# Decode attention: P times V spread over four column strips of TensorE, heads folded by four matmuls

## The chip, the cores and the metric

The kernel runs on one core of a Trainium2 chip. The core has TensorE (PE, with its weight loads shown apart as PEld), VectorE (DVE), ScalarE (ACT), GpSimd (POOL), SyncE (SP, which only issues transfers here) and 16 DMA engines that bring data from HBM into SBUF, the on-chip memory of 128 partitions. Matmul results land in PSUM, a second memory of 128 partitions with eight banks of 512 fp32 columns each. The metric is the device time of one execution in microseconds, lower is better.

## The reference

One token is decoded. Two branches share the input x (1 x 512) and are mixed by a gate:

```python
g = sigmoid((x * gate_w).sum(-1, keepdims=True))
# A: attention over a cache, H = 32 heads, Sk = 65536 positions, Dh = 128
q = (x @ wq) split into heads
p = softmax(q . k_cache * Dh**-0.5)
a = (p @ v_cache, heads side by side) @ wo
# B: feed-forward, F = 1792
b = (silu(x @ w_gate) * (x @ w_up)) @ w_down
out = g * a + (1 - g) * b
```

All tensors are bf16. The K and V caches are 512 MiB each, and every byte of them is needed once; all the weights together are some 13 MB.

## The kernel before

**Tiling.** Of each head's 65536 positions, partition p holds positions 512p to 512p + 511, so a head is 512 columns of positions, "blocks", each with 128 values. `CUTS` divides them into three tiles of 168, 168 and 176 blocks, 96 tiles in all (N = 32 x 3) for K and 96 for V. A tile is 5,376 or 5,632 KB. Four ring slots in SBUF (`SLOTS`, line 18) hold whatever K and V tiles are in flight or in work; a slot's next load waits until the last reader of the slot's old tile is done.

**Order.** Everything is issued in an order written out by hand (`manual_schedule`, line 80; the loop from line 555 and the tail from line 608). SP issues all loads (`load`, line 139, the transfer itself at line 147). A step n of the loop loads K tile n and a V tile v that lags by three to five tiles (`LEAD`, `SKIPS`), and then issues, per engine in this order:

- if a head's last V tile was done in the step before: the head's sum of P times V (`head_diagonal`);
- the products of K with q on DVE (`products`: line 304 multiplies in place, line 308 adds halves until 16 columns are left);
- in the first step of a head, in the middle of the DVE work, the previous head's maximum, its spread over the partitions by a matmul (line 363), and its exponentials on ACT (line 374), which write P_sb, 128 x 512 in bf16;
- the head's row (`head_row`), which scales the 128 sums by the gate over the softmax's total and puts them into a row;
- P times V for tile v (`values`, line 401): one matmul for every four blocks, 42 or 44 in a tile;
- the rest of the score sums (`scores`, line 325: PE adds the 16 columns over an identity matrix), after which the K slot is free.

**P times V.** For blocks j to j+3 the stationary operand is P_sb[:, j:j+4] (128 x 4) and the moving operand is the four blocks of V (128 x 512). The 4 x 512 result in PSUM holds P of block c' times V of block c; only c = c' is wanted, that is, row c in columns 128c to 128c + 127. All 128 matmuls of a head add into the same four partitions of one bank, and two such banks take turns by head.

**A head's sum.** For 30 of the heads `head_diagonal` copies the four wanted pieces to SBUF with four activations, each of which multiplies its 4 x 128 columns by a column of the identity (zeroing the other rows); one fp32 matmul with ones adds the four partitions into a row of 512, and DVE adds its four parts of 128 (line 444). For the last two heads `head_copy` and `head_column` bring the unmasked 4 x 512 to SBUF and pick the rows with four matmuls against columns of the identity, giving a column.

**The end.** After the last step the remaining V tiles arrive in smaller pieces (`V_CUTS`), then the tiles of wo (`load_wo`, line 237); `project` (line 513) multiplies the heads' sums by wo as its pieces arrive, one activation copies the result and SP stores it.

Of the kernel before, what the change touches and what calls it, by code (L numbers as in the profile page):

```python
# [8 lines left out]
ACT = mybir.ActivationFunctionType  # L9
ALU = mybir.AluOpType  # L10
AXIS = mybir.AxisListType
P = 128
# [23 lines left out]
def kernel(  # L36
# [14 lines left out]
    nc = tc.nc  # L51
    bf16 = mybir.dt.bfloat16
    f32 = mybir.dt.float32

    _, H, Sk, Dh = A_k_cache.shape
# [5 lines left out]
    NBH = Sk // P  # L61
# [4 lines left out]
    scale = float(Dh) ** -0.5  # L66
# [4 lines left out]
    consts = ctx.enter_context(tc.tile_pool(name="consts", bufs=1))  # L71
    small = ctx.enter_context(tc.tile_pool(name="small", bufs=2))
    ppool = ctx.enter_context(tc.tile_pool(name="ppool", bufs=2))
    psum_s = ctx.enter_context(tc.tile_pool(name="psum_s", bufs=2, space=bass.MemoryType.PSUM))
    psum_o = ctx.enter_context(tc.tile_pool(name="psum_o", bufs=2, space=bass.MemoryType.PSUM))
    psum_a = ctx.enter_context(tc.tile_pool(name="psum_a", bufs=1, space=bass.MemoryType.PSUM))
    psum_r = ctx.enter_context(tc.tile_pool(name="psum_r", bufs=1, space=bass.MemoryType.PSUM))
    psum_m = ctx.enter_context(tc.tile_pool(name="psum_m", bufs=2, space=bass.MemoryType.PSUM))
# [20 lines left out]
    ident_f = consts.tile([P, P], f32, name="ident_f")  # L99
# [3 lines left out]
    ones_f = consts.tile([P, P], f32, name="ones_f")  # L103
# [7 lines left out]
    for t in range(KT):  # L111
        nc.tensor.matmul(
            x_ps[:, t : t + 1],
            lhsT=x_row.rearrange("o (p t) -> o t p", t=KT)[:, t, :],
            rhs=one_b,
            start=True,
            stop=True,
        )
    nc.scalar.activation(out=xT, in_=x_ps, func=ACT.Copy)
    for t in range(KT):  # L120
        nc.vector.tensor_copy(out=X_bc[:, t, :], in_=xT[:, t : t + 1].to_broadcast([P, P]))

    rowsum = consts.tile([P, 1], f32, name="rowsum")
    oT = consts.tile([P, 2 * H + 1], bf16, name="oT")
    nc.vector.memset(oT, 0.0)
# [4 lines left out]
    rg = consts.tile([P, H], f32, name="rg")  # L130
    a_ps = psum_a.tile([1, D], f32, name="a_ps")

    S_parts = {}
    K_tiles, V_tiles, S_tiles, P_tiles, O_tiles = {}, {}, {}, {}, {}

    def span(n):
        return CUTS[n % G], CUTS[n % G + 1]

    def load(dst, cache, n, name, cuts=None):
        h = n // G  # L140
        a, b = span(n)
        t, taken[name, n] = big(name)
        view = t[:, : (b - a) * Dh].rearrange("p (j d) -> p j d", d=Dh)
        src = cache[0, h, :, :].rearrange("(p j) d -> p j d", p=P)
        cuts = cuts or (0, b - a)
        for c, d in zip(cuts[:-1], cuts[1:]):
            nc.sync.dma_start(out=view[:, c:d, :], in_=src[:, a + c : a + d, :])
        dst[n] = view
# [30 lines left out]
    WG = 4  # L179
# [157 lines left out]
    def add_up(n):  # L337

        h = n // G
        a, b = span(n)  # L340
        if a == 0:
            S_tiles[h] = consts.tile([P, NBH], f32, name="S_sb")
        nc.vector.tensor_reduce(  # L343
            out=S_tiles[h][:, a:b], in_=S_parts.pop(n), axis=AXIS.X, op=ALU.add
        )
# [47 lines left out]
    def values(n, lo=0, hi=None):  # L393

        h = n // G
        a, b = span(n)
        hi = b - a if hi is None else hi
        if a + lo == 0:
            O_tiles[h] = psum_o.tile([4, 4 * Dh], f32, name="O_ps")
        for j in range(lo, hi, 4):  # L400
            nc.tensor.matmul(  # L401
                O_tiles[h],
                lhsT=P_tiles[h][:, a + j : a + j + 4],
                rhs=V_tiles[n][:, j : j + 4, :],
                start=(a + j == 0),
                stop=(a + j == NBH - 4),
            )
        if hi == b - a:
            del V_tiles[n]
            free.append(taken.pop(("V_t", n)))  # L410

    def head_copy(h):
        O_ps = O_tiles.pop(h)
        O_sb = small.tile([4, 4 * Dh], f32, name="O_sb")
        nc.scalar.activation(out=O_sb, in_=O_ps, func=ACT.Copy)
        return [O_sb[:, c * Dh : (c + 1) * Dh] for c in range(4)]

    def head_column(h, O_parts):
        oh_ps = psum_m.tile([P, 1], f32, name="oc_ps", tag="misc")
        for c in range(4):  # L420
            nc.tensor.matmul(
                oh_ps, lhsT=O_parts[c], rhs=ident_f[0:4, c : c + 1], start=(c == 0), stop=(c == 3)
            )
        nc.scalar.activation(
            out=oT[:, 2 * h + 1 : 2 * h + 2], in_=oh_ps, func=ACT.Copy, scale=rg[:, h : h + 1]
        )

    def head_diagonal(h):
        O_ps = O_tiles.pop(h)
        O_sb = small.tile([4, 4 * Dh], f32, name="O_sb")  # L430
        for c in range(4):
            nc.scalar.activation(  # L432
                out=O_sb[:, c * Dh : (c + 1) * Dh],
                in_=O_ps[:, c * Dh : (c + 1) * Dh],
                func=ACT.Copy,
                scale=ident_f[0:4, c : c + 1],
            )
        r_ps = psum_r.tile([1, 4 * Dh], f32, name="r_ps")
        nc.tensor.matmul(r_ps, lhsT=ones_f[0:4, 0:1], rhs=O_sb, start=True, stop=True)  # L439
        return r_ps  # L440

    def head_row(h, r_ps):
        r_sb = consts.tile([1, Dh], f32, name="r_sb")
        nc.vector.tensor_reduce(  # L444
            out=r_sb, in_=r_ps.rearrange("o (c d) -> o d c", c=4), axis=AXIS.X, op=ALU.add
        )
        if h < WG:
            for a, b, s, at in pieces:
                lo, hi = max(a, h * Dh), min(b, h * Dh + Dh)
                if lo < hi:  # L450
                    nc.scalar.activation(
                        out=tall_rows[s][:, at + lo - a : at + hi - a],
                        in_=r_sb[:, lo - h * Dh : hi - h * Dh],
                        func=ACT.Copy,
                        scale=rg[0:1, h : h + 1],
                    )
            return
        if h % WG == 0:
            rows[h // WG] = small.tile([1, WG * Dh], bf16, name="o_row")
        at = (h % WG) * Dh  # L460
        nc.scalar.activation(  # L461
            out=rows[h // WG][:, at : at + Dh], in_=r_sb, func=ACT.Copy, scale=rg[0:1, h : h + 1]
        )

    def turn_first():
# [57 lines left out]
    def fold_copy():  # L523
        a_sb = small.tile([4, 4 * Dh], f32, name="O_sb")[0:1, :]
        nc.scalar.activation(out=a_sb, in_=a_ps, func=ACT.Copy)
        fold["a"] = psum_a.tile([2, D // 2], f32, name="a_ps")
        return a_sb
# [11 lines left out]
    rows = {}  # L539
# [15 lines left out]
    for n, v in steps:  # L555
        if n > 1:
            load(K_tiles, A_k_cache, n, "K_t")
        if v is not None:
            load(V_tiles, A_v_cache, v, "V_t", V_CUTS.get(v))
            for half in range(2):  # L560
                if n - half in TALL_LOADS:
                    load_tall(TALL_LOADS[n - half], half)
            if n == N - 1:
                load(V_tiles, A_v_cache, v + 1, "V_t", V_CUTS.get(v + 1))
        size = span(n)[1] - span(n)[0]
        cuts = (0, size // 2, size) if n == 0 else (0, size)
        top_of = None
        if n % G == 0 and n > 0:
            top_of = n // G - 1
            cuts = (0, 64, size)  # L570
        vector = (i for a, b in zip(cuts[:-1], cuts[1:]) for i in products(n, a, b))
        r_ps = None
        if done is not None:
            r_ps = head_diagonal(done)
        if top_of is not None:
            next(vector, None)
            add_up(top_of * G + G - 1)
            exponentials(top_of, row_max(top_of))
        for _ in vector:
            pass  # L580
        if n == FOLD:
            a_sb = fold_copy()
        if n % G:
            add_up(n - 1)
        if r_ps is not None:
            head_row(done, r_ps)
        if n == 2:
            feed_forward_out(*ff)
        if v is not None:
            values(v)  # L590
        if group is not None:
            (turn if group else lambda g: turn_first())(group)
        if n == 1:
            ff = feed_forward_in()
        scores(n)
        if n == 1:
            ff = feed_forward_mid(*ff)
            free.append(gu_slot)
        if group:
            late.append(group)  # L600
        if n in TALL_PROJECTS:
            project_tall(TALL_PROJECTS[n])
        if n == FOLD:
            fold_in(a_sb)
        group = done // WG if done is not None and done % WG == WG - 1 else None
        done = v // G if v is not None and v % G == G - 1 else None
# [12 lines left out]
    O_parts = head_copy(H - 2)  # L619
# [8 lines left out]
    O_parts = head_copy(H - 1)  # L628
# [39 lines left out]
```

## Time and profile before

| | |
|---|---|
| time, median of 3 runs | 2522.24 us (2522.07 to 2522.47) |
| span of the profiled execution | 2520.4 us |
| PE busy | 1408.6 us (56%), weight loads 488.2 us |
| DVE busy | 2234.4 us (89%) |
| ACT busy | 103.4 us (4%) |
| transfer queue of SP | 1087.65 MB, 99.9% of the 16 engines' span |
| HBM read | 1087.64 MB, 432 GB/s over the span |
| mean granted TensorE clock | 0.734 of full |

The profiled execution's own time is not listed apart from its span; the runs' median is 1.8 us above that span. The span runs from the first to the last instruction. The digits of the page's slices are busy tenths of one fortieth of the span each. In a group's line stand the line of code, the engine, the operation, what it writes and reads, shapes and count, then busy time and the mean of one in ns, and behind the bar the idle time of the engine just before these instructions and what ended it. In the chain of waits each row is a start, a length and what the time went to; a DMA row lasts from the issue of the transfer to its landing, queueing included.

### The profile page before, as it was taken

Reading aid. Unit: us, or ns where it says so; the run is one execution under the profiler, and the core shown is the slowest. Engines: PE = TensorE matmul, PEld = TensorE weight load, DVE = VectorE, ACT = ScalarE, POOL = GpSimd, SP = SyncE. Lnnn points to the kernel's source line nnn. Section 1 sums busy time; section 2 is a strip of 40 time slices with the busy share of each in tenths; the row PEclk is TensorE's granted clock in tenths of the full one; section 3 lists DMA queues with packets and bytes.
Section 4 is the critical chain, followed back from the end, with each engine's and each line's share of the span. In section 5 each row is a group of like instructions: output and inputs, shape, how many; then the busy total and the mean of one; then the engine's idle time right before and its main releaser. Section 6 shows DMA issues by size and latency. Waiting matters only on the chain.

```text
span 2520.4 us, 12122 instructions
## 1 busy us (share of the span) xinstructions
PE 1408.6 (56%) x5174; PEld 488.2 (19%) x5174; DVE 2234.4 (89%) x788; ACT 103.4 (4%) x314; POOL 0.7 (0%) x6
## 2 busy tenths in 40 slices
PE   2555546565555654655546565554564655556468
PEld 1111112121121211211212121111121211112123
DVE  7999998988989889999889998889999889898880
ACT  1000000000000000000000000000000000000000
POOL 0000000000000000000000000000000000000000
PEclk7677767676776766677767777776677777777779
DMA  9999999999999999999999999999999999999999
GB/s 420 430 439 433 433 431 435 431 433 434 434 432 436 433 434 433 432 434 433 431 434 435 435 433 431 434 433 433 433 433 433 436 434 434 433 432 431 434 434 390
DMA packets 31101, 1088.41 MB, mean 432 GB/s; under 512 B 3532, under 2 KB 4048, under 8 KB 5192
## 3 DMA queue, kind: packets, MB, share of 16 engines
q1 hardware_dynamic: 31046, 1087.65, 99.9%
q8 instruction: 40, 0.66, 0.1%
q14 instruction: 13, 0.11, 0.0%
q10 hardware_dynamic: 2, 0.00, 0.0%
HBM read 1087.64 MB, written 0.00 MB: 432 GB/s over the span
## 4 chain that ended last, share of the span: by engine, by line
DMA 59%; DVE 23%; PE 17%; issue 1%; ACT 0%; SPq 0%; DVEq 0%
DMA V_t<-in_A_v_cache_dram 45%; DMA K_t<-in_A_k_cache_dram 14%; PE O_ps L401 13%; DVE K_t L304 11%; DVE K_t L308 10%; PE part_ps L325 3%; DVE S_sb L343 0%; PE mT_ps L363 0%; DVE m L358 0%; DMA wo_t<-in_A_wo_dram 0%; ACT diag L360 0%; DVE top L370 0%; DVE rg L391 0%; PE a_ps L291 0%; DVE recip L390 0%
## 5 line engine op out<-in xcount | busy, mean ns | idle before, releaser
L401 PE MATMUL O_ps<-V_t,P_sb 128*4 128x512 bf16 x4096 | 1087.3, 434 | 777.8 <-DMA V_t<-in_A_v_cache_dram 774.9
L304 DVE TENSOR_TENSOR K_t<-K_t,q_bc 128x22528 bf16<-128x22528 bf16 (+4 forms) x128 | 1111.9, 8686 | 163.5 <-DMA K_t<-in_A_k_cache_dram 163.1
L308 DVE TENSOR_TENSOR K_t<-K_t 128x5376 bf16<-128x5376 bf16 (+11 forms) x384 | 1016.3, 2647 | 12.2
L401 PEld LDWEIGHTS <-P_sb 128*4 128x4 bf16 x4096 | 383.5, 94 | 1492.8 <-issue 1082.7
L325 PE MATMUL part_ps<-K_t,ident_b 128*128 128x504 bf16 (+2 forms) x640 | 228.8, 506 | 167.9 <-DVE K_t L308 167.9
L325 PEld LDWEIGHTS <-ident_b 128*128 128x128 bf16 x640 | 62.5, 109 | 310.8 <-issue 211.5
L363 PE MATMUL mT_ps<-diag,ones_f 128*128 128x129 f32 (+1 forms) x64 | 24.9, 491 | 130.3 <-ACT diag L360 130.3
L432 ACT ACTIVATE O_sb<-O_ps,ident_f 4x128 f32<-4x128 f32 x120 | 33.2, 346 | 1002.9 <-PE O_ps L401 1002.9
L343 DVE TENSOR_REDUCE S_sb<-part_ps 128x168 f32<-128x504 f32 (+1 forms) x96 | 59.8, 623 | 3.2 <-PE part_ps L325 3.2
L370 DVE TENSOR_REDUCE top<-mT_ps 128x1 f32<-128x128 f32 x32 | 9.3, 292 | 44.8 <-PE mT_ps L363 44.8
L363 PEld LDWEIGHTS mT_ps<-diag,ones_f 128*128 128x128 f32 x64 | 15.6, 303 | 154.6 <-ACT diag L360 154.2
L461 ACT ACTIVATE o_row<-r_sb,rg 1x128 bf16<-1x128 f32 x26 | 10.4, 401 | 581.3 <-DVE r_sb L444 581.3
L439 PE MATMUL r_ps<-O_sb,ones_f 4*1 4x512 f32 x60 | 33.0, 630 | 0.0
L360 ACT ACTIVATE diag<-ident_f,m 128x128 f32<-128x128 f32 x32 | 12.8, 401 | 428.1 <-DVE m L358 428.1
L374 ACT ACTIVATE P_sb<-S_sb,bias 128x512 bf16<-128x512 f32 x32 | 23.1, 722 | 1.0
L358 DVE TENSOR_REDUCE m<-S_sb 128x1 f32<-128x512 f32 x32 | 22.0, 686 | 1.1
L444 DVE TENSOR_REDUCE r_sb<-r_ps 1x128 f32<-1x512 f32 x30 | 20.1, 670 | 0.0
L156 PE MATMUL qg_ps<-wq_t,X_bc 128*128 128x512 bf16 x32 | 9.2, 460 | 10.7 <-DMA wq_t<-in_A_wq_dram 10.7
L390 DVE RECIPROCAL recip<-tot_ps 128x1 f32<-128x1 f32 x1 | 0.2, 168 | 16.6 <-PE tot_ps L385 16.6
L291 PE MATMUL a_ps<-O_sb,ones_f 1*1 1x512 f32 x2 | 1.9, 1030 | 19.7 <-ACT O_sb L290 19.7
L372 ACT ACTIVATE bias<-top 128x1 f32<-128x1 f32 x32 | 6.5, 203 | 41.2 <-DVE top L370 41.2
L246 PEld LDWEIGHTS <-gu_t 128*128 128x128 bf16 x112 | 6.9, 157 | 0.6 <-issue 0.6
(68 smaller groups left out, 88.5 us busy)
## 6 DMA issues: line engine op xcount, KB each, us to landing
K_t<-in_A_k_cache_dram SPq DMA_DIRECT2D x63, 5376.0 KB
V_t<-in_A_v_cache_dram SPq DMA_DIRECT2D x62, 5376.0 KB
K_t<-in_A_k_cache_dram SPq DMA_DIRECT2D x32, 5632.0 KB
V_t<-in_A_v_cache_dram SPq DMA_DIRECT2D x31, 5632.0 KB
V_t<-in_A_v_cache_dram SPq DMA_DIRECT2D x2, 2816.0 KB
K_t<-in_A_k_cache_dram SPq DMA_DIRECT2D x2, 2688.0 KB
V_t<-in_A_v_cache_dram SPq DMA_DIRECT2D x2, 2560.0 KB
wq_t<-in_A_wq_dram SPq DMA_DIRECT2D x1, 4096.0 KB
```

Source lines behind the costliest of these rows:

```text
L304: yield nc.vector.tensor_tensor(out=K, in0=K, in1=q_rep, op=ALU.mult)
L308: yield nc.vector.tensor_tensor(out=K[:, :, 0:half], in0=K[:, :, 0:half], in1=K[:, :, half : 2 * half], op=ALU.add,)
L325: nc.tensor.matmul(part[:, :, 0:take], lhsT=ident_b, rhs=K_tiles[n][:, :, c : c + take], start=(i == 0), stop=(i == len(takes) - 1),)
L343: nc.vector.tensor_reduce(out=S_tiles[h][:, a:b], in_=S_parts.pop(n), axis=AXIS.X, op=ALU.add)
L358: nc.vector.tensor_reduce(out=m, in_=S_tiles[h], axis=AXIS.X, op=ALU.max)
L360: nc.scalar.activation(out=diag[:, :P], in_=ident_f, func=ACT.Copy, scale=m)
L363: nc.tensor.matmul(mT_ps[:, :wide], lhsT=ones_f, rhs=diag[:, :wide], start=True, stop=True)
L374: nc.scalar.activation(out=P_tiles[h], in_=S_tiles[h], func=ACT.Exp, bias=bias, scale=scale, accum_out=new_sum(h),)
L401: nc.tensor.matmul(O_tiles[h], lhsT=P_tiles[h][:, a + j : a + j + 4], rhs=V_tiles[n][:, j : j + 4, :], start=(a + j == 0), stop=(a + j == ...
L432: nc.scalar.activation(out=O_sb[:, c * Dh : (c + 1) * Dh], in_=O_ps[:, c * Dh : (c + 1) * Dh], func=ACT.Copy, scale=ident_f[0:4, c : c + 1],)
L439: nc.tensor.matmul(r_ps, lhsT=ones_f[0:4, 0:1], rhs=O_sb, start=True, stop=True)
L444: nc.vector.tensor_reduce(out=r_sb, in_=r_ps.rearrange("o (c d) -> o d c", c=4), axis=AXIS.X, op=ALU.add)
```

## The change

The two PSUM banks for P times V become fixed tiles of 128 partitions, cleared once at the start by DVE. The matmul for blocks j to j+3 now writes partitions 32s to 32s + 3 with s = (j / 4) mod 4, so successive matmuls go to the four column strips of the array in turn, and each strip has its own accumulation over a quarter of the head. A constant `pick` (128 x 4) has a one in row 32s + c of column c, for all four s.

A head's sum is then: one activation copies all 128 x 512 to SBUF, and four fp32 matmuls, one for each c, multiply column c of `pick` with columns 128c to 128c + 127 and add up in one row of 128 in PSUM. The masking activations, the matmul with ones and the DVE reduction go away, and `head_row` reads its values from PSUM. The last two heads use the same `pick` in `head_column`.

```diff
-    psum_o = ctx.enter_context(tc.tile_pool(name="psum_o", bufs=2, space=bass.MemoryType.PSUM))
+    psum_o = ctx.enter_context(tc.tile_pool(name="psum_o", bufs=1, space=bass.MemoryType.PSUM))
...
+    pick = consts.tile([P, 4], f32, name="pick")
+    nc.vector.tensor_reduce(
+        out=pick,
+        in_=ident_f.rearrange("p (j q) -> p q j", q=32)[:, 0:4, :],
+        axis=AXIS.X,
+        op=ALU.add,
+    )
+    O_banks = []
+    for i in range(2):
+        O_banks.append(psum_o.tile([P, 4 * Dh], f32, name=f"O_ps{i}"))
+        nc.vector.memset(O_banks[i], 0.0)
...
-        if a + lo == 0:
-            O_tiles[h] = psum_o.tile([4, 4 * Dh], f32, name="O_ps")
         for j in range(lo, hi, 4):
+            strip = (a + j) // 4 % 4
             nc.tensor.matmul(
-                O_tiles[h],
+                O_banks[h % 2][32 * strip : 32 * strip + 4, :],
                 lhsT=P_tiles[h][:, a + j : a + j + 4],
                 rhs=V_tiles[n][:, j : j + 4, :],
-                start=(a + j == 0),
-                stop=(a + j == NBH - 4),
+                start=(a + j < 16),
+                stop=(a + j >= NBH - 16),
             )
...
     def head_copy(h):
-        O_ps = O_tiles.pop(h)
-        O_sb = small.tile([4, 4 * Dh], f32, name="O_sb")
-        nc.scalar.activation(out=O_sb, in_=O_ps, func=ACT.Copy)
+        O_sb = small.tile([P, 4 * Dh], f32, name="O_sb")
+        nc.scalar.activation(out=O_sb, in_=O_banks[h % 2], func=ACT.Copy)
...
-                oh_ps, lhsT=O_parts[c], rhs=ident_f[0:4, c : c + 1], start=(c == 0), stop=(c == 3)
+                oh_ps, lhsT=O_parts[c], rhs=pick[:, c : c + 1], start=(c == 0), stop=(c == 3)
...
-    def head_diagonal(h):
-        O_ps = O_tiles.pop(h)
-        O_sb = small.tile([4, 4 * Dh], f32, name="O_sb")
+    def head_sum(O_parts):
+        r_ps = psum_r.tile([1, Dh], f32, name="r_ps")
         for c in range(4):
-            nc.scalar.activation(
-                out=O_sb[:, c * Dh : (c + 1) * Dh],
-                in_=O_ps[:, c * Dh : (c + 1) * Dh],
-                func=ACT.Copy,
-                scale=ident_f[0:4, c : c + 1],
-            )
-        r_ps = psum_r.tile([1, 4 * Dh], f32, name="r_ps")
-        nc.tensor.matmul(r_ps, lhsT=ones_f[0:4, 0:1], rhs=O_sb, start=True, stop=True)
+            nc.tensor.matmul(
+                r_ps, lhsT=pick[:, c : c + 1], rhs=O_parts[c], start=(c == 0), stop=(c == 3)
+            )
         return r_ps

     def head_row(h, r_ps):
-        r_sb = consts.tile([1, Dh], f32, name="r_sb")
-        nc.vector.tensor_reduce(
-            out=r_sb, in_=r_ps.rearrange("o (c d) -> o d c", c=4), axis=AXIS.X, op=ALU.add
-        )
...
-            out=rows[h // WG][:, at : at + Dh], in_=r_sb, func=ACT.Copy, scale=rg[0:1, h : h + 1]
+            out=rows[h // WG][:, at : at + Dh], in_=r_ps, func=ACT.Copy, scale=rg[0:1, h : h + 1]
...
-            r_ps = head_diagonal(done)
+            r_ps = head_sum(head_copy(done))
```

## The prediction, made before the run

> **What bounds the kernel now.** I read the page's slices and transfer queues first, then busy time by stretch, then the chain of waits at both ends, then the groups of instructions. The page's slices and queues:
>
> ```profile
> PE   2555546565555654655546565554564655556468
> DVE  7999998988989889999889998889999889898880
> DMA  9999999999999999999999999999999999999999
> ...
> q1 hardware_dynamic: 31046, 1087.65, 99.9%
> ```
>
> TensorE (PE) is half busy and VectorE (DVE) nearly full, but the DMA row has no slice under 9, and the one transfer queue that matters holds the 16 engines for 99.9% of the span. Busy time by stretch (us; then PE, weight loads, DVE, ScalarE (ACT), GpSimd, TensorE's granted clock, DMA share, GB/s) shows where even that lets go:
>
> ```profile
> 0.00:60.00 60.00, 18.83 (x154) 11.50 (x155) 42.90 (x24) 6.84 (x13) 0.70 (x6) 0.73 0.98 417
> 960.00:1020.00 60.00, 26.09 (x94) 9.32 (x94) 58.33 (x20) 1.42 (x4) 0.00 (x0) 0.66 1.00 431
> 2400.00:2460.00 60.00, 35.70 (x137) 12.13 (x136) 51.71 (x16) 1.91 (x6) 0.00 (x0) 0.77 1.00 434
> 2460.00:2520.00 60.00, 53.91 (x281) 24.01 (x279) 0.85 (x5) 3.14 (x9) 0.00 (x0) 1.00 0.92 388
> ```
>
> Only the first and the last stretch are below a share of 1. Adding up the trace's single packets, the first large one starts at 1.8 us, the last ends near 2517.3, and between 15 and 2510 us the 16 engines lose 0.13 us of their time together. A 43,008-byte packet takes 1,590 ns (16,000 of them); 1,589.6 with PE idle all through it, 1,590.5 with PE busy all through it. So the body is 1,088 MB at a fixed 433 GB/s. The chain of waits near the end:
>
> ```profile
> 2406.77 37.02 DMA V_t<-in_A_v_cache_dram
> 2443.79 0.04 issue
> 2443.83 11.17 PE O_ps L401 x42
> 2455.00 0.02 issue
> 2455.02 21.44 DMA V_t<-in_A_v_cache_dram
> ...
> 2508.75 8.19 DMA wo_t<-in_A_wo_dram
> 2516.95 0.04 issue
> 2516.99 1.05 PE a_ps L513 x8
> ```
>
> PE stands in this chain because a burst of P times V frees the slot that the next load waits for. But 37.02 us from issue to landing, for a load whose 5,632 KB need 13.3 us, says that 23.7 us of older transfers were still ahead of it: the slot came free long before the DMA engines needed it. Bytes issued less bytes landed, over 433 GB/s, gives that reserve at each load: in the body (130 to 2400 us) 10.0 us at the least and 12.4 at the median for K loads, 11.3 and 22.2 for V loads; before that it is lowest at the K load issued at 110.11 us, 5.2 us. The very end is the last wo transfer, eight matmuls, a copy and the store.
>
> **The change part by part.** The profiled execution has a span of 2520.4 us; the median of the runs is 2522.24, so 1.8 us lie around the span. I take that 1.8 as fixed.
>
> ```profile
> L401 PE MATMUL O_ps<-V_t,P_sb 128*4 128x512 bf16 x4096 | 1087.3, 434 | 777.8 <-DMA V_t<-in_A_v_cache_dram 774.9
> L401 PEld LDWEIGHTS <-P_sb 128*4 128x4 bf16 x4096 | 383.5, 94 | 1492.8 <-issue 1082.7
> L432 ACT ACTIVATE O_sb<-O_ps,ident_f 4x128 f32<-4x128 f32 x120 | 33.2, 346 | 1002.9 <-PE O_ps L401 1002.9
> L439 PE MATMUL r_ps<-O_sb,ones_f 4*1 4x512 f32 x60 | 33.0, 630 | 0.0
> L444 DVE TENSOR_REDUCE r_sb<-r_ps 1x128 f32<-1x512 f32 x30 | 20.1, 670 | 0.0
> ```
>
> *P times V.* 4096 matmuls keep their shape; their outputs rotate over four strips. Now a burst of 42 takes 11.17 us. If the strips overlap, what is left is bounded below by the weight loads, 42 x 94 ns = 3.9 us; if they don't, it stays 11.2. No row shows two strips at once, so these are the ends, with a worse one under the rivals. I take about 4.5 us, near the weight-load row, because each strip has weights and outputs of its own. A burst then ends some 6.7 us earlier, PE's 777.8 us of waiting for V grow by about 96 x 6.7 = 640, and V slots are handed back 6.7 us earlier. That lengthens a reserve of 22 us and moves nothing, since the packets already run back to back. What is late next is what is late now: the landing of V and K.
>
> *The head's sum.* Gone, 30 times: four scaled copies on ACT (1.11 us for the four together in the timeline at 1022 us), two passes over 512 columns on PE (2 x 0.63 = 1.26) and the DVE reduction (0.67). Added: one copy of 128x512, which costs what the end's 4x512 copy does (0.58 us) since columns and not partitions set the time (128x512 into q_bc is 0.60); four fp32 matmuls, eight passes of 128 columns. By the column matmuls of the last heads (eight passes in 1.05 us) up to the 128x129 pass (0.49 us x 8 = 3.9) that is 1.0 to 3.9 us; I take 1.3, as most rows with such small weights stand near the first. ACT gains 0.5 us a head, DVE 20.1 us in all, PE loses 0 to 2.6 us a head, in idle time of a step of 25 us. DVE's 20 us turn into waiting for K (now 163.1 us of idle before L304). The rows are read by ACT straight from PSUM, so ACT's wait for the DVE reduction (581 us) becomes a wait for PE; behind it on ACT stands only the next head's copy and exponentials, which wait for later work anyway. r_ps has one buffer, so the next sum on PE waits for the row's copy, three steps (75 us) after it. No DMA and no instruction of SP or GpSimd moves. Path: 0.
>
> *The start.* DVE clears two PSUM banks of 512 and forms pick. The 128x128 clear of ones_f took 0.17 us, the 128x504 PSUM reduction 0.675, so 2 x 0.6 + 0.2 = 1.4 us, between 3.6 and 5.8 us of the span; DVE is then free until K lands at 19.47 us, a cover of 13.7 us. The first use of the banks is at 98.97 us. Path: 0. With the cover gone it would be 1.4 us.
>
> *The end.* The last V piece lands at 2508.7; its five matmuls end at 2510.2 and would end up to 0.6 us earlier. That gains nothing: projecting then follows seven wo tiles of which the last landed piece comes at 2517.6. Here the clock matters. In the body the granted clock is 0.64 to 0.77 on average: in the burst at 2443.83 the first ten weight loads are 0.43 us apart and the following 31 take 6.56 us, so the clock goes to full about 4 us into a burst. In the last 60 us PE is dense (53.91 of 60) and the clock is 1.00. If strips shrink 214 matmuls from 46 us to 15 to 20, PE is no longer dense there and the last eight projections (0.109 us apart) may run at half clock: 8 x 0.109 = 0.87 us more. From 2510 on seven groups at half clock need 1.74 us each against 1.24 us between landings, so PE is dense again for over 4 us before the last one; I take 0.2 us, the ends being 0 and 0.9.
> [...]
>
> *Sum.* Body 0, start 0, head's sums 0, end +0.2: span 2520.6, time 2522.24 + 0.2 = 2522.4 us. Bounds of the unknowns that leave the DMA engines fed: -0.1 (the lost 0.13 us) and +0.9.
>
> **Rivals.**
> (1) *Strips neither overlap nor pipeline* (slower). If a change of strip made each matmul wait for the one before, it would cost its whole duration, 379 ns at full clock at the median, instead of 216 between starts. In the body a burst takes some 10 x 0.634 + 32 x 0.379 = 18.5 us, and the step (25 us) still holds it. In the end stretch V lands 42 matmuls' worth in 12.7 us, 302 ns each: beyond that spacing PE decides. From 2457.4 on, 214 x 0.379 = 81.1 us, 2.2 us of other PE work, then copy, column and 56 projections 7.7 us and 2.4 us to the end of the span give about 2551: 2552.6 us, 1.2% slower. For it: nothing before uses more than one strip. Against: PE takes the weights of the next matmul while one runs (weight loads lie beside matmuls in every burst).
> [...]
> (2) *The change doesn't do what it says*: strips take turns at 216 ns, as now. 2522.2 us.
> (3) *Half clock at the end*: 2522.24 + 0.9 = 2523.1 us.
> (4) *Four streams disturb the transfers.* PE busy costs a packet 0.9 ns of 1,590 now; four times that over the 17% of the span that bursts would fill (96 x 4.5 us) is 0.23% x 17% = 1.0 us: 2523.2. Only packets 1.2% longer in the bursts (19 ns) would reach 0.2%.
> (5) *Faster by more than a trace.* It would need the loads to be starved today; 0.13 us of lost DMA time in the body leaves no room, and the 1.8 us of the start and 3.1 us after the last landing are not touched.
>
> **How the numbers follow.** A measurement of this kernel can tell about 0.2% (5.0 us) from no change: under 2517.2 is faster, over 2527.3 slower. Forecast 0.60; (2) 0.13; (3) 0.16; (4) 0.04, of which 0.01 beyond 0.2%; (1) 0.05; (5) 0.02. So faster 0.02, same 0.92, slower 0.06. The range covers the forecast's ends, (2), (3) and the small form of (4), 2522.1 to 2524.1 with both ends of the clock and the packets added, and I give it 1.2 us more on each side for a packet time that moves by half a thousandth: 2520.9 to 2525.3. It leaves out (1), (5) and the large (4), 0.08.
>
> **What would show it.** Right: DMA share 1.00 in every stretch but the first and last; bursts of 42 in 4 to 6 us; granted clock near 0.5 to 0.6 in the body; L444's group gone; DVE's idle before L304 up by some 20 us; V loads longer from issue to landing, not the span shorter. Wrong: matmuls of a burst more than 302 ns apart at the end, a DMA share under 0.99 in any middle stretch, or packets above 1,600 ns.

## The result, and the profile after

The changed kernel takes 2526.55 us (median of 20 runs, 2523.59 to 2527.26) against 2522.32 us for the kernel before on the same chips (20 runs, 2522.07 to 2522.49). The ratio is 1.0015, 95% interval 1.0009 to 1.0021: slower by 4.2 us, 0.17%. That is within the 0.2% that the prediction took as no change, but the range ended at 2525.3 us and the time is 1.2 us above it. The spread is new, too: the kernel before stays within 0.4 us, the changed one has 16 runs between 2525.9 and 2527.3 and four between 2523.6 and 2523.9.

The page's slices and transfer queues of the changed kernel (its profiled execution: span 2524.9 us, time 2526.66 us):

```profile
PE   2333223333233332333333332332332323232335
...
PEclk7656556555555555556555565555565655555566
DMA  9999999999999999999999999999999999999998
...
q1 hardware_dynamic: 31046, 1087.65, 99.7%
q8 instruction: 42, 0.69, 0.1%
```

PE fell from fives and sixes to twos and threes, and the granted clock with it, from sixes and sevens to fives and sixes; in the last slice it fell from nine tenths to six. The DMA row has its only digit under 9 in the last slice. q8 is the fetching of instructions: 42 packets of 16 KB, where the kernel before has 40.

The costliest groups:

```profile
L412 PE MATMUL O_ps<-V_t,P_sb 128*4 128x512 bf16 x4096 | 430.4, 590 | 839.3 <-DMA V_t<-in_A_v_cache_dram 836.4
L337 PE MATMUL part_ps<-K_t,ident_b 128*128 128x504 bf16 (+2 forms) x640 | 252.9, 550 | 687.4 <-DVE K_t L320 687.4
L425 ACT ACTIVATE O_sb<-O_ps 128x512 f32<-128x512 f32 x32 | 19.1, 597 | 993.0 <-PE O_ps L412 993.0
L441 PE MATMUL r_ps<-O_sb,pick 128*1 128x128 f32 x240 | 51.4, 387 | 0.0
```

P times V is busy for 430 us instead of 1,087 although a single matmul is now longer (590 ns against 434): four run at a time. A burst of 44 at 1010 us takes 4.27 us, one of 42 at 1036 us takes 4.81; over the trace bursts of 42 take 3.0 to 4.9 us, 4.5 at the median. In these bursts four matmuls start within 14 ns and the next four 0.38 to 0.43 us later (0.22 at full clock), which is the spacing of single ones at half clock before (0.43 us between starts). The strips do overlap.

Busy time by stretch (columns as before):

```profile
960.00:1020.00 60.00, 14.55 (x103) 4.68 (x101) 58.33 (x20) 2.02 (x5) 0.00 (x0) 0.56 1.00 431
2400.00:2460.00 60.00, 21.73 (x158) 7.23 (x159) 51.84 (x18) 1.93 (x5) 0.00 (x0) 0.60 1.00 434
2460.00:2520.00 60.00, 30.04 (x231) 11.98 (x227) 0.33 (x2) 2.23 (x7) 0.00 (x0) 0.60 0.93 389
```

From 60 to 2460 us the DMA share is 0.99 to 1.02 in every stretch and the rate is that of before; nothing was lost or won there. (The first 60 us have 0.98 in both kernels.) The last 60 us have the clock at 0.60 instead of 1.00 and PE busy for 30 instead of 54 us. The chain of waits ends so:

```profile
2482.79 28.78 DMA wo_t<-in_A_wo_dram
2511.57 0.04 issue
2511.61 1.86 PE a_ps L513 x8
2513.47 1.80 PE oc_ps L431 x8
2515.27 7.24 PE a_ps L513 x48
2522.50 0.02 issue
2522.53 0.37 ACT out_sb L636
```

Before, PE waited for wo until 2516.95 and needed 1.05 us after it. Now PE waits for nothing after 2511.61: eight projections take 1.86 us instead of 1.05, the column 1.80 instead of about 1.0, and the 48 others come one after the other. By the trace's clock records full clock returns only at 2519.1 us. PE has become the bound of the last ten microseconds. A second thing is in the first line: that piece of wo is complete at 2511.57, on 15 engines it had landed by 2509.93 and on one 1.6 us later.

### The profile page after: what moved, and what is told of

Read it like the earlier page. It is cut to its first block, busy times and chain, and to the rows that moved or that the text cites. A ratio compares the mean times of both kernels' runs of the same rounds, so it can differ in the third digit from the quotient of the medians.

```text
span 2524.9 us, 12385 instructions
## 1 busy us (share of the span) xinstructions
PE 806.8 (32%) x5354; PEld 271.1 (11%) x5354; DVE 2218.7 (88%) x761; ACT 85.5 (3%) x224; POOL 0.7 (0%) x6
## 4 chain that ended last, share of the span: by engine, by line
DMA 61%; DVE 31%; PE 7%; issue 1%; ACT 0%; SPq 0%; DVEq 0%
DMA V_t<-in_A_v_cache_dram 32%; DMA K_t<-in_A_k_cache_dram 28%; DVE K_t L316 16%; DVE K_t L320 14%; PE O_ps L412 4%; PE part_ps L337 2%; DMA wo_t<-in_A_wo_dram 1%; DVE S_sb L355 0%; PE a_ps L513 0%; PE mT_ps L375 0%; DVE m L370 0%; ACT diag L372 0%; DVE top L382 0%; PE a_ps L303 0%; PE oc_ps L431 0%
## 5 line engine op out<-in xcount | busy, mean ns | idle before, releaser
L316 DVE TENSOR_TENSOR K_t<-K_t,q_bc 128x22528 bf16<-128x22528 bf16 (+4 forms) x128 | 1112.1, 8688 | 178.4 <-DMA K_t<-in_A_k_cache_dram 177.6
L412 PE MATMUL O_ps<-V_t,P_sb 128*4 128x512 bf16 x4096 | 430.4, 590 | 839.3 <-DMA V_t<-in_A_v_cache_dram 836.4
L337 PE MATMUL part_ps<-K_t,ident_b 128*128 128x504 bf16 (+2 forms) x640 | 252.9, 550 | 687.4 <-DVE K_t L320 687.4
L412 PEld LDWEIGHTS <-P_sb 128*4 128x4 bf16 x4096 | 133.1, 115 | 1126.0 <-issue 1095.6
L337 PEld LDWEIGHTS <-ident_b 128*128 128x128 bf16 x640 | 71.7, 121 | 854.5 <-DVE K_t L320 506.5
L425 ACT ACTIVATE O_sb<-O_ps 128x512 f32<-128x512 f32 x32 | 19.1, 597 | 993.0 <-PE O_ps L412 993.0
L441 PE MATMUL r_ps<-O_sb,pick 128*1 128x128 f32 x240 | 51.4, 387 | 0.0
L441 PEld LDWEIGHTS r_ps<-O_sb,pick 128*1 128x1 f32 x240 | 24.2, 110 | 37.1 <-issue 22.8
L461 ACT ACTIVATE o_row<-r_ps,rg 1x128 bf16<-1x128 f32 x26 | 9.2, 354 | 196.3 <-PE r_ps L441 196.3
L231 PE MATMUL a_ps<-tall_sb,tallT 44*1 44x512 bf16 (+2 forms) x22 | 10.2, 617 | 0.0
L513 PE MATMUL a_ps<-wo_t,oT 128*2 128x256 bf16 x56 | 9.2, 339 | 0.2 <-DMA wo_t<-in_A_wo_dram 0.2
```

Of the source, the lines that this page charges most:

```text
L231: nc.tensor.matmul(a_ps, lhsT=tallT[s][:K, a + t : a + t + 1], rhs=tall_sb[:K, t, :], start=False, stop=(r == len(TALL_ROUNDS) - 1 and t = ...
L316: yield nc.vector.tensor_tensor(out=K, in0=K, in1=q_rep, op=ALU.mult)
L337: nc.tensor.matmul(part[:, :, 0:take], lhsT=ident_b, rhs=K_tiles[n][:, :, c : c + take], start=(i == 0), stop=(i == len(takes) - 1),)
L412: nc.tensor.matmul(O_banks[h % 2][32 * strip : 32 * strip + 4, :], lhsT=P_tiles[h][:, a + j : a + j + 4], rhs=V_tiles[n][:, j : j + 4, :], ...
L425: nc.scalar.activation(out=O_sb, in_=O_banks[h % 2], func=ACT.Copy)
L441: nc.tensor.matmul(r_ps, lhsT=pick[:, c : c + 1], rhs=O_parts[c], start=(c == 0), stop=(c == 3))
```

## The experiments

Two theories for the 4.2 us. Theory 1: PE made thin by the strips runs at half clock at the end, and the projections become the bound; beside it a late DMA engine. Theory 2: the strips don't matter, and the longer program alone does it, 180 more matmuls and their weight loads being two more instruction fetches. A third, that strips cost something in the body, was kept as a rival. All medians below are of 11 runs, beside the kernel before on the same chip (2522.29, 2522.34 and 2522.33 us in the three sets). Behind each ratio stands its 95% interval. For steps of some 1.1 us these intervals include 1; what carries those steps is that five different programs show them, 1.0 to 1.2 us each, and that not one run of the five lies as low as 2523.1 us. The edits are shown shortened to what they do.

**one_strip: the new sum without strips.**

```diff
-            strip = (a + j) // 4 % 4
+            strip = 0
...
-                start=(a + j < 16),
-                stop=(a + j >= NBH - 16),
+                start=(a + j < 4),
+                stop=(a + j >= NBH - 4),
```

> The changed kernel, but all matmuls of P times V go to strip 0; the head's sum stays with four matmuls, so the instruction count is that of the changed kernel. Theory 1 (strips thin out PE's work at the end, the clock falls to half there and the last projections make the end late): clock 1.00 in the last 60 us, 2522.3 to 2522.6 us, or up to 2523.9 if the engine that lands last is delayed by an instruction fetch as in the changed kernel's trace. Theory 2 (it is the longer code alone, whose fetches delay the last data): 2523.9 to 2526.5 us, the same late landing as in the changed kernel.

Measured: 2523.39 us (2523.23 to 2523.68), ratio 1.0004 (0.9995 to 1.0013). Without strips 3.2 of the 4.2 us are gone and so is most of the spread; 1.1 us stay.

**strips_last2 and strips_but_last2: strips for the last two heads alone, and for the other thirty alone.**

```diff
-            strip = (a + j) // 4 % 4
+            spread = h >= H - 2            # strips_last2; h < H - 2 in strips_but_last2
+            strip = (a + j) // 4 % 4 if spread else 0
```

(The start and stop of each sum follow, as above. In strips_but_last2 the last two columns read rows 0 to 3 only, as before the change.)

> Strips for the last two heads alone, one strip for the other thirty. Theory 1: the body's clock returns to 0.73, the end's is at about 0.6, and the whole loss is there: 2525.0 to 2526.6 us. Theory 2: 2523.9 to 2526.5, no matter where the strips are. Theory 3 (the strips cost in the body): 2522.3 to 2522.6 us.

> Strips for thirty heads, one strip for the last two. Theory 1: body clock about 0.57, end clock 1.00, 2522.3 to 2522.6 us (2523.9 with a late engine). Theory 2: as the changed kernel, 2526.5. Theory 3: 2525.0 to 2526.6 us.

Measured: 2526.05 us (2523.51 to 2527.53), ratio 1.0014 (1.0005 to 1.0022), for the last two heads; 2523.49 us (2523.19 to 2523.95), ratio 1.0005 (0.9996 to 1.0014), for the other thirty. Two heads of 32 carry what the strips cost, as far as the spread of the runs can tell; theory 3 falls, and so does theory 2 as the whole account, which asked for 2526.5 us with strips in thirty heads.

**strips_warm: strips everywhere, PE kept dense at the end.**

```diff
+            if n >= N - 4 and strip == 3:
+                for _ in range(5):
+                    nc.tensor.matmul(
+                        warm[0],
+                        lhsT=P_tiles[h][:, a + j : a + j + 4],
+                        rhs=V_tiles[n][:, j : j + 2, :],
+                        start=True,
+                        stop=True,
+                    )
```

> The changed kernel with five idle matmuls of 256 columns, on data already landed and into a PSUM bank nobody reads, behind each fourth matmul of the last four V tiles, so that PE is as dense there as before. Theory 1: the clock is 1.00 in the last 60 us although the strips stay, 2522.3 to 2522.6 us (2523.9 with a late engine). Theory 2: at least 2526.5, since the code is longer still. Theory 3: 2526.5.

Measured: 2523.48 us (2523.37 to 2523.76), ratio 1.0005 (0.9996 to 1.0013). The kernel has more work for PE than the changed one and is 3.1 us faster. Its last 60 us by stretch, and the end of its chain of waits:

```profile
2460.00:2520.00 60.00, 45.45 (x467) 29.26 (x462) 0.33 (x2) 2.54 (x8) 0.00 (x0) 0.91 0.93 389
```

```profile
2510.09 8.19 DMA wo_t<-in_A_wo_dram
2518.28 0.04 issue
2518.33 1.05 PE a_ps L523 x8
2519.37 0.02 issue
2519.40 0.37 ACT out_sb L647
```

The clock is 0.91 over the stretch and 1.00 in its parts from 2500 to 2510 and from 2510 to 2520 us; the last eight projections are back at 1.05 us, and the transfer is the bound again, only 1.3 us later than before. So with strips, the clock makes the difference of 3.1 us. What the three kernels without a cold end share is 1.1 to 1.2 us, and a program as long as the changed one's, or longer. The next set goes after that.

**before_longer and before_longer4: the kernel before with idle matmuls of one column.**

```diff
         r_ps = psum_r.tile([1, 4 * Dh], f32, name="r_ps")
+        for _ in range(6):                 # 4 in before_longer4
+            nc.tensor.matmul(
+                r_ps[:, 0:1], lhsT=ident_b[0:4, 0:1], rhs=ident_b[0:4, 0:1], start=True, stop=True
+            )
```

> The kernel before with six matmuls of one column ahead of each head's sum, into a place that the sum overwrites: TensorE's program is as long as in the changed kernel, everything else as before. Theory 1 (a longer program brings a further instruction fetch, which delays the engine whose data land last by some 1.2 us): 42 fetches, the last landing of wo at about 2518.9 in the span, 2523.2 to 2523.7 us, clock 1.00 at the end. Theory 2 (the 1.1 us that one_strip and strips_but_last2 keep come from the copies of 128 partitions and the four fp32 matmuls at the end): 40 to 42 fetches, 2522.2 to 2522.5 us.

> As before_longer with four extra matmuls a head, 240 instructions in all instead of 360. If what counts is whether the 41st instruction fetch comes before the last data, it comes near 2500 us here and delays the last landing: 2523.0 to 2523.6 us. If the loss grows with the number of instructions: about 2523.0, two thirds of the 1.04 us of before_longer. If the fetch falls on an engine that runs ahead: 2522.3.

Measured: 2523.38 us (2523.26 to 2523.88), ratio 1.0004 (0.9996 to 1.0013), and 2523.48 us (2523.20 to 2524.86), ratio 1.0006 (0.9997 to 1.0015). PE is half idle and four or six matmuls of one column a head are next to no work; the chain of before_longer shows where it goes:

```profile
2476.49 33.29 DMA V_t<-in_A_v_cache_dram
2509.78 0.02 issue
2509.80 8.17 DMA wo_t<-in_A_wo_dram
2517.97 0.04 issue
2518.01 1.06 PE a_ps L517 x8
```

The last V piece is issued at 2476.49 (before: 2476.47) and lands 33.29 us later, where it took 32.27: the same bytes behind the same queue, 1.0 us later. Its page has 42 instruction fetches for 40. What a fetch goes with can be followed packet by packet in the traces of the changed kernel, which has 42 as well, and of the kernel before. In the changed kernel one 16 KB fetch comes at 2486.6 us. It is one packet, took 0.96 us, and from the load that lands at 2490.9 us on, one of the 16 parts of every load lands 1.6 to 2.4 us after ten of the others. (A packet's record does not name its engine; which one had the fetch is read from the parts' landings.) In the kernel before the last two fetches come at 2474 and 2499 us and fall on engines whose parts landed some 1.5 us ahead of the load's last one; those come closer to the others and the load as a whole is not late. By the pages and the chains of waits the same split runs through all twelve programs but before_width8, where PE is the bound. In five of the seven with 41 to 43 fetches the last V piece takes 33.29 to 33.66 us from issue to landing, against 32.27 in the kernel before (40 fetches) and 32.24 in strips_but_last2_old_sum (40). In the other two, the changed kernel and strips_last2, the wo piece of the chain takes 28.78 and 28.71 us, against 27.39 in strips_old_sum (40) and 27.26 in before_thin_end (39). Four extra matmuls (41 fetches) cost as much as six (42), 33.52 and 33.29 us for the same V piece, so the number of instructions is not the price. That it counts whether a fetch before the last data falls on an engine that lands last is read from the landings of the two traces above; no run tests it alone. Three runs with four extra matmuls lie at 2524.7 to 2524.9 us; they have no profile, and what they lost is open.

**strips_old_sum and strips_but_last2_old_sum: the strips with the sum of before**, so that the program has its old length.

```diff
+    def head_sum(h):
+        for c in range(4):
+            nc.scalar.activation(..., in_=O_banks[h % 2][:, c * Dh : (c + 1) * Dh],
+                func=ACT.Copy, scale=pick[:, c : c + 1])
+        r_ps = psum_r.tile([1, 4 * Dh], f32, name="r_ps")
+        nc.tensor.matmul(r_ps, lhsT=ones_f[:, 0:1], rhs=O_sb, start=True, stop=True)
...
+        nc.vector.tensor_reduce(
+            out=r_sb, in_=r_ps.rearrange("o (c d) -> o d c", c=4), axis=AXIS.X, op=ALU.add
+        )
```

> The changed kernel with strips for all heads, but the head's sum by four masked copies, one matmul with ones over 128 partitions and the VectorE reduction, as long a TensorE program as before. Theory 1: 40 fetches and no late engine, the half clock at the end stays: 2523.0 to 2525.5 us. Theory 2: 2526.2 to 2526.7 us, as the changed kernel, if the program's length does not matter and the 1.1 us lie in the last two heads' copy and column.

> As strips_old_sum, with one strip for the last two heads. Theory 1: neither cost is left, so the strips of thirty heads bring and cost nothing: 2522.1 to 2522.5 us, last landing at 2517.6. Theory 2: 2523.3 to 2523.6 us.

Measured: 2525.28 us (2522.44 to 2526.15), ratio 1.0010 (1.0001 to 1.0019), and 2522.30 us (2522.05 to 2522.55), ratio 1.0000 (0.9991 to 1.0009). The first has 40 fetches, a last piece that is not late (the one of 27.39 us) and the cold end: 2.9 us. The end of its chain, in a run of 2526.15 us:

```profile
2482.73 27.39 DMA wo_t<-in_A_wo_dram
2510.13 0.04 issue
2510.17 1.87 PE a_ps L522 x8
2512.03 1.80 PE oc_ps L431 x8
2513.83 8.13 PE a_ps L522 x48
```

The second has neither cost and is the kernel before to within 0.04 us, with strips in thirty heads. Its stretches and the end of its chain:

```profile
960.00:1020.00 60.00, 14.74 (x104) 4.71 (x102) 58.33 (x20) 2.56 (x8) 0.00 (x0) 0.56 1.00 431
2460.00:2520.00 60.00, 54.00 (x281) 24.01 (x279) 0.85 (x5) 3.17 (x9) 0.00 (x0) 1.00 0.92 388
```

```profile
2508.77 8.20 DMA wo_t<-in_A_wo_dram
2516.97 0.04 issue
2517.01 1.05 PE a_ps L524 x8
```

PE needs 11 us less in a stretch of the body than before, at a lower clock, and the end is the old one to 0.02 us.

**before_thin_end: a thin PE without strips.** The kernel before, leaving out three of four P times V matmuls of the last four V tiles.

```diff
         for j in range(lo, hi, 4):
+            if n >= N - 4 and (a + j) % 16 and a + j < NBH - 4:
+                continue
```

> The kernel before, one strip, but of the last four V tiles only every fourth matmul of P times V is computed (and the very last one); the other sums are left out. PE is as thin at the end as with strips, without a strip or a new instruction. Theory 1 (a thin PE loses its clock at the end, strips or not): clock about 0.6 in the last 60 us, single runs between 2522.3 and 2526, median 2524 to 2526 us. Rival (the strips themselves slow the end, for instance by a drain or their column matmuls): 2522.0 to 2522.5 us.

Measured: 2525.35 us (2524.84 to 2525.95), ratio 1.0012 (1.0003 to 1.0021). Less work, no strip, and 3.0 us slower. Its last stretch and the end of its chain:

```profile
2460.00:2520.00 60.00, 37.27 (x153) 16.15 (x152) 0.85 (x5) 2.77 (x8) 0.00 (x0) 0.69 0.92 388
```

```profile
2509.94 1.87 PE a_ps L515 x8
2511.80 1.79 PE oc_ps L423 x8
2513.60 6.98 PE a_ps L515 x48
```

About the same lengths as in the changed kernel (1.86, 1.80, 7.24), so the cold end needs no strip at all, and the column over 128 rows costs no more than the one over four.

**before_width8: fewer instructions.** The kernel before with `WIDTH = 8`, one more halving on DVE and half of the score matmuls.

> The kernel before with one more halving of the products on VectorE (8 columns left, not 16), so that TensorE sums them with 320 matmuls instead of 640; VectorE gets 96 additions of some 0.86 us, 82 us more, to about 92% busy. Theory 1: 640 fewer TensorE instructions are two to three fetches fewer, and the last data land earlier: 2520.8 to 2522.2 us, if VectorE still keeps up. Theory 2: 2522.2 to 2522.5 us. If VectorE becomes the bound in places: above 2523.

Measured: 2523.23 us (2522.59 to 2524.90), ratio 1.0005 (0.9996 to 1.0013): a miss, and no test of the fetches. DVE is 92% busy, the DMA share stays at 1.00 in the body, but the chain ends differently:

```profile
2470.36 0.04 issue
2470.40 12.48 PE O_ps L401 x44
...
2489.14 22.97 PE O_ps L401 x106
2512.11 0.87 PE a_ps L513 x8
2512.99 0.98 PE oc_ps L421 x8
2513.96 5.34 PE a_ps L513 x48
```

PE itself is the bound from 2470.40 us on, without a wait. Its burst of 44 there takes 12.48 us where it took 9.66 before: the granted clock from 2460 to 2520 us is 0.94, which is some 7 us at half clock, where the kernel before has full clock from 2447.77 us to the end. The V tile ahead of the burst landed 0.6 us later (2470.36 against 2469.74 us); that PE's longer idle time before it cost the clock is not shown. The last head's scores are not late (its maximum goes through PE at 2461.95 us, before at 2462.23). PE reaches the column 1.90 us later than before (2512.92 against 2511.02). So this kernel, too, paid for a clock lost near the end. There are 38 fetches for 40, but with PE as the bound the time says nothing of what they are worth.

## Why the prediction was wrong

The account that the runs give: 2.9 us (strips_old_sum) to 3.0 (before_thin_end) for the half clock at the end, 1.0 to 1.2 us for one more instruction fetch ahead of the last data; together 3.9 to 4.2, measured 4.2.

*The body.* Right. The packets keep their 1,590 ns, the DMA share is 1.00, bursts of 42 take 4.5 us at the median (forecast 4.5), and the faster slots only lengthen the reserve. But that shows at the K loads, whose median reserve rises from 12.4 to 19.2 us, and hardly at the V loads (22.2 to 23.2), where the prediction looked for it: the slot that a burst frees is taken by the next K load (the burst that ends at 1014.56 us is followed by a K load at 1014.61). That nothing is to be had there is shown by strips_but_last2_old_sum. One detail was off: PE's idle time does not gather before V (774.9 to 836.4 us) but before the scores (167.9 to 687.4), since scores stand behind the burst in PE's queue and the wait moves to whatever comes next. And the weight loads were no lower bound: bursts of 42 go down to 3.0 us, under the 3.9 of the prediction, for the loads overlap each other too (4096 of 115 ns keep PEld busy for 133 us).

*The start.* Right: clearing the banks took 1.03 us and pick 0.17, ending at 4.84 us, far ahead of the first K.

*The head's sum on the engines.* Right as a cost of engine time. Eight passes take 1.86 us in most heads, at half clock, and 1.24 at the least (taken: 1.3, ends 1.0 to 3.9), the copy 0.60 us. DVE's idle before its products rises by 14.5 us (163.1 to 177.6) where 20 were forecast; it had 20 us less to do.

*The end.* Here is the first failed step: "I take 0.2 us, the ends being 0 and 0.9." The mechanism was named and its direction right; the term was mis-sized, 0.2 for 2.9, and the upper end was wrong as well. It was priced on the last eight projections alone. What stands on PE after the last V piece is the column and all 56 projections, 64 instructions, 0.213 us apart at half clock and 0.109 at full: 13.6 us against 7.0, in 8.8 us between that landing and wo's last. At full clock PE keeps up with wo; at half it does not, and every group's lateness is carried on to the next. The prediction even had the numbers, 1.74 us of work for 1.24 us of landings, but drew from them that PE would be dense for 4 us and the clock up in time.
In the bursts of the kernel before the clock took 1.5 to 6.0 us of work to come back, 4.1 at the median (91 bursts), and the prediction had carried these 4 us over to the end. There it took longer. From the first of the eight projections to full clock the changed kernel needs 7.5 us (2511.6 to 2519.1). The others have a granted clock of 0.62 (strips_last2), 0.65 (before_thin_end) and 0.53 (strips_old_sum) from 2510 to 2520 us, which puts full clock some 6.3, 7.0 and 9.3 us after their first projection. PE was busy all that time. In the traces of the kernel before and of the changed one the clock records change only at multiples of 3.41 us from one another (184 and 207 changes), whatever PE begins when; why the end took longer than the bursts stays open. The spread of the runs may come from here too, the 2.9 us not being lost where full clock returns early enough; that is the author's guess. That the four runs near 2523.7 are of this kind is argued from their time (before plus one late fetch), not seen in a profile; before_thin_end has no such run among its eleven.

*What the prediction left out.* The second failed step is in "The head's sum": "Path: 0." The sum of the step held PE, ACT, DVE and the transfers' issues, but not the program itself. 180 more matmuls, each with its weight load, are 360 instructions; they moved the fetches and brought two more (42 for 40), and one that came ahead of the last data, at 2486.6 us, fell by the landings on an engine which lands last (its parts come 1.6 to 2.4 us after ten of the others): 1.1 us by one_strip. Which engine it would fall on could not be read from the lines of the profile before. The profile before showed the queue (40 fetches), and it was read as 0.1% of the engines' span and passed over. The share is right, and says nothing of one engine at the one moment when all 16 must be done.

*The rivals.* (1) fell: strips overlap, four starting within 14 ns. (2) fell for the same reason. (3) was the right one with the wrong price (2523.1 instead of 2525.3). (4) fell: packets with PE idle took 1,590.5 ns and with PE busy 1,589.2. (5) fell. "Same", at 0.92, came true by 0.8 us, and partly by luck: two terms put at 0.2 and 0 made 3.9 to 4.2 of the 5.0 us that it allows. The range was too narrow at the top because (3)'s ceiling was taken as a bound when it was a guess at how much PE work the clock touches, and because no term stood for the fetches.

## What to carry to other kernels

The transfers ran without a gap here (DMA share 0.99 to 1.02 from 60 to 2460 us), and a faster engine in the body was worth nothing (11 us less PE work in 60 left the time within 0.04 us); the end was the one place where it acted. So list everything that still has to run after the last bulk transfer, and price all of it at the clock that the engine will have there, not at the one it has now. Making matmuls shorter, or leaving some out, lowered the clock of the ones behind them here (0.60 and 0.69 over the last 60 us instead of 1.00), and keeping the last stretch dense brought it back (0.91, 3.1 us faster). Count the instruction fetches with the transfers too: five programs that had 41 to 43 of them instead of 40 were 1.0 to 1.2 us slower here, and by the landings of two traces it is the engine on which a fetch falls that decides.

## What the runs showed of the hardware that was not expected

- Four column strips with 128 x 4 weights and 512 columns run four at a time: starts within 14 ns, four in the 0.43 us that one took at the same half clock, a burst of 42 in 4.5 us at the median against 11.2.
  That is 2.5 times over a whole burst (the two medians), with the lower clock already in it (0.56 against 0.66 from 960 to 1020 us).
- The granted clock is 0.5 or 1.0 in every record of the kernel before and of the changed one, and its changes there lie multiples of 3.41 us apart. After a thin stretch at the end it took some 6.3 to 9.3 us of unbroken PE work to come back (four profiles), against 1.5 to 6.0 us in the bursts of the kernel before.
- A 16 KB instruction fetch is one packet, and by the landings on one engine; it takes 0.88 to 0.97 us in these two kernels, and one data packet of each, which starts as a fetch ends, took longer (22,528 bytes took 1,305 ns in the changed kernel, at 2487.5 us, and 1,331 ns in the kernel before, at 2474.6 us, instead of 836 at the median). The 16 engines do not run level: late in the kernel before five of them land their parts of a load 1.3 to 7 us ahead of the other eleven, and the two fetches that fell on engines some 1.5 us ahead (2474 and 2499 us) did not make a load late.
